# Retention and gated MLP in one kernel: b divided out of w_sg and put back at the output, the middle row tile of two batches mixed on TensorE's row halves, w_in loaded by SyncE in columns, and an engine listed for each cast and copy

## The chip, the cores and the metric

One core of one Trainium2 chip. The metric is the device time of one execution in microseconds (us), here the median of three runs; lower is better.

## The reference

q, k and v are f32 of 8 batches x 8 heads x 576 positions x 64. Each head's scores are masked and damped by a power of the distance, without softmax, and multiplied with v; the 8 heads side by side make x (8 x 576 x 512), which goes through a gated MLP that mixes over positions:

```
ret = (q @ k.T / 8) * Dmat            # Dmat = gamma_h ** (i - j) for j <= i, else 0
x   = concat_heads(ret @ v)
h   = gelu_tanh(x @ w_in)             # 512 -> 1024; u = h[:512], v = h[512:]
v_n = (v - mean) / sqrt(var + 1e-6) * g_ln
v_s = w_sg @ v_n + b_sg               # over positions, 576 x 576; b_sg one number a position
out = x + (u * v_s) @ w_out
```

## The kernel before, in words

**Tiles.** A pair of batches has 2 x 576 = 1152 rows, which are 9 row tiles of 128; tile 4 (MID) holds the last 64 rows of the one batch and the first 64 of the other. There are 4 pairs. The attention runs over 36 steps i of its own, 9 a pair: a step takes 256 rows of 4 heads (two such steps make two row tiles), or the middle tile of all 8 heads.

**Attention of a step.** SP loads q, k and v (L317). The damping is split into a factor on q and one on v: POOL multiplies q and v (L515, L518) and casts k to bf16 (L511; ACT does the first four, L509). PE transposes q and k (L531), DVE copies them out of PSUM (L534); from step 20 on the DMA transposes them instead (L523). PE makes the scores in 64x64 tiles (L556), DVE masks them (L570), PE multiplies with v (L689) and adds what earlier rows bring through a running state (L681; the state is summed by L589 and kept block diagonal in zbdA and zbdB, which ACT, DVE and POOL fill). This lands in p_oz, of which there is one; ACT copies it to xT (L719), x with its features on the partitions.

**MLP of a row tile.** mlp_V (L756): 4 matmuls of 512 columns with the second half of w_in (L762), gelu on ACT (L765), mean and variance on DVE (L770 to L772), the power -0.5 on POOL (L775), a last product on DVE (L777) and the normalised vn on ACT (L787). mlp_U (L791): the same with the first half of w_in, turned (L802), gelu to uT on ACT (L807). batch(b) (L812), once all vn of a batch are there: 8 groups of 5 matmuls of 288 columns mix the positions (L824), and DVE multiplies each with uT (L832). Of the middle tile each batch has only 64 rows; the other 64 rows of vmid hold 1/g_ln and the matching rows of wT hold b_sg, so that the same matmul brings the bias in (L405 to L439 make both, with transposes on PE). Then 4 matmuls of 512 columns with w_out a row tile (L851; g_ln is multiplied into w_out, L478). x is added in the first half of the tiles by 4 transposing matmuls on PE (L854), and ACT copies the sum out (L865); in the last 18 (late) the DMA transposes x (L844) and DVE adds it (L861). SP writes the tile (L869).

**Weights.** w_in comes by 4 DMAs that POOL issues and that cast on the way (L329). w_sg comes by SP (L445), POOL casts it (L447), PE transposes it in 25 pieces (L454), DVE and ACT copy them to wT (L460 to L466). A copy that is shifted by 64 rows, for the odd batches, is made by 3 DMAs from SBUF to SBUF (L469).

**What sets the order.** Every piece of work is a unit of the class Plan (L116): an engine, a planned cost, what it reads and writes. TURN (L19) gives each unit its place in one sequence by hand, and the units are issued in that sequence, so that on each engine the order is fixed. The planned costs only choose PSUM banks (4 of them, p_d, for all MLP work and the transposes) and put 30 matmuls on zeros (L292) into gaps at the start.

## Time and profile before

| what | value |
|---|---|
| runs | 209.09, 209.66, 211.18 us; median 209.66 |
| span of the profiled execution, first to last instruction | 208.7 us |
| mean granted TensorE clock | 0.992 |
| busy: PE, DVE, ACT, POOL | 197.3, 161.3, 136.9, 125.0 us |
| moved by DMA | 48.93 MB, 234 GB/s on average |

The profile is of one execution, whose span is 208.7 us; the runs' times are 0.4 to 2.5 us above that, since they also hold what lies ahead of the first and behind the last instruction and differ from run to run. PE is the engine of the matmuls and PEld its weight loads; a matmul's end is modelled, so the starts of rows, not their lengths, tell what one costs in a stream. DVE, ACT and POOL are VectorE, ScalarE and GpSimd; SPq is the queue of SyncE. "x4" in a row is the number of instructions that were merged into it.

### The profile page before, as it was taken

What the parts mean: (1) busy time and instruction counts of PE and PEld (TensorE: products, weight loads), DVE (VectorE), ACT (ScalarE), POOL (GpSimd) and SP (SyncE); (2) the same over time, 40 slices, a digit from 0 to 9 for tenths busy, and PEclk for the clock granted to TensorE, in tenths of its full rate; (3) what the DMA queues carried; (4) which work ended last, traced back from release to release, by engine and by line L of the source; (5) the groups of instructions that cost most, each with busy time, mean ns of one, the idle gap of its engine ahead of it and who ended that gap; (6) DMA issues with size and microseconds to landing.
All of it is one profiled execution on the core that took longest, in us unless ns stands there. A gap on an engine that the chain in (4) does not pass through costs nothing.

```text
span 208.7 us, 7251 instructions
## 1 busy us (share of the span) xinstructions
PE 197.3 (95%) x2892; PEld 127.1 (61%) x2892; DVE 161.3 (77%) x440; ACT 136.9 (66%) x304; POOL 125.0 (60%) x186
## 2 busy tenths in 40 slices
PE   7779799999997999999999999999999999999992
PEld 2354568668675676667565667566657556664651
DVE  1383969879997998877987798557999998787573
ACT  5428468886778448886578677994785498644400
POOL 4965999998991897853869229635766563103000
PEclk9969999999999999999999999999999999999999
DMA  5999999999999999999999997999999999697655
GB/s 160 302 188 254 224 284 305 289 314 275 193 219 223 316 279 284 300 266 230 131 327 221 204 195 225 132 239 273 249 208 259 216 221 189 136 316 181 175 162 216
DMA packets 99073, 48.93 MB, mean 234 GB/s; under 512 B 42848, under 2 KB 93344, under 8 KB 99040
## 3 DMA queue, kind: packets, MB, share of 16 engines
q1 hardware_dynamic: 97808, 47.30, 99.9%
q0 software_dynamic: 1088, 1.05, 3.4%
q8 instruction: 22, 0.36, 0.8%
q14 instruction: 11, 0.09, 0.2%
q10 hardware_dynamic: 144, 0.13, 0.2%
HBM read 32.79 MB, written 9.44 MB: 202 GB/s over the span
## 4 chain that ended last, share of the span: by engine, by line
PE 84%; POOL 4%; issue 3%; DMA 3%; DVE 2%; ACT 1%; SPq 1%; DVEq 0%; POOLq 0%
PE p_d L824 19%; PE p_d L851 15%; PE p_d L762 15%; PE p_d L802 14%; PE p_oz L689 5%; PE p_s L556 4%; PE p_d L531 3%; PE p_oz L681 3%; DMA qkf<-in_q_dram 3%; PE p_d L854 2%; PE p_oz L589 1%; SPq L317 1%; PE p_d L454 1%; POOL qkb L515 1%; DVE ret L570 1%
## 5 line engine op out<-in xcount | busy, mean ns | idle before, releaser
L570 DVE TENSOR_TENSOR ret<-p_s,tri 128x512 bf16<-128x512 f32 x64 | 42.5, 683 | 6.5 <-PE p_s L556 6.1
L775 POOL TENSOR_TENSOR stat<-stat,mhalf 128x1 f32<-128x1 f32 x36 | 19.8, 551 | 38.9 <-DVE stat L772 37.0
L515 POOL TENSOR_TENSOR qkb<-qkf,gq 128x512 bf16<-128x512 f32 x35 | 36.8, 1057 | 9.2 <-DMA qkf<-in_q_dram 9.2
L518 POOL TENSOR_TENSOR vb<-vf,gv 128x512 bf16<-128x512 f32 x36 | 37.9, 1058 | 6.4 <-DMA vf<-in_v_dram 5.7
L824 PE MATMUL p_d<-wT,vn 128*128 128x288 bf16 x256 | 40.6, 286 | 0.0
L802 PE MATMUL p_d<-xT,w_in 128*128 128x512 bf16 (+2 forms) x224 | 36.1, 303 | 0.0
L762 PE MATMUL p_d<-w_in,xT 128*128 128x512 bf16 x144 | 36.1, 380 | 0.0
L851 PE MATMUL p_d<-w_out,uT 128*128 128x512 bf16 (+1 forms) x148 | 35.9, 374 | 0.0
L719 ACT ACTIVATE xT<-p_oz 128x256 bf16<-128x256 f32 x64 | 24.4, 453 | 16.5 <-PE p_oz L689 11.1
L832 DVE TENSOR_TENSOR uT<-p_d,uT 128x288 bf16<-128x288 f32 x64 | 27.5, 452 | 9.4 <-PE p_d L824 8.0
L765 ACT ACTIVATE vg<-p_d 128x512 f32<-128x512 f32 x36 | 21.4, 595 | 15.7 <-PE p_d L762 14.9
L824 PEld LDWEIGHTS <-vn 128*128 128x128 bf16 x256 | 24.3, 98 | 8.2
L787 ACT ACTIVATE vn<-vg,stat 128x512 bf16<-128x512 f32 x32 | 25.6, 811 | 3.1 <-DVE stat L777 2.0
L770 DVE BATCH_NORM_STATS2 stat<-vg 128x6 f32<-128x512 f32 x36 | 24.6, 684 | 2.6 <-ACT vg L765 2.4
L807 ACT ACTIVATE uT<-p_d 128x512 bf16<-128x512 f32 x36 | 21.1, 594 | 6.0 <-PE p_d L802 5.8
L511 POOL CAST qkb<-qkf 128x512 bf16<-128x512 f32 x32 | 19.5, 612 | 9.1 <-PE p_oz L589 4.7
L802 PEld LDWEIGHTS <-w_in 128*128 128x128 bf16 x224 | 18.5, 98 | 10.3 <-issue 0.2
L851 PEld LDWEIGHTS <-uT 128*128 128x128 bf16 x148 | 13.9, 98 | 13.7
L762 PEld LDWEIGHTS <-xT 128*128 128x128 bf16 x144 | 13.0, 98 | 12.8 <-ACT xT L719 0.2
L534 DVE COPY qkT<-p_d 128x1024 bf16<-128x1024 bf16 x20 | 13.6, 682 | 6.4 <-PE p_d L531 6.2
L824 PE MATMUL p_d<-wT,vmid 128*128 128x288 bf16 x64 | 18.3, 287 | 0.0
L556 PE MATMUL p_s<-qkT 64*64 64x128 bf16 (+1 forms) x576 | 15.3, 218 | 3.1 <-DVE qkT L534 1.4
(96 smaller groups left out, 280.3 us busy)
## 6 DMA issues: line engine op xcount, KB each, us to landing
out_dram<-ob SPq DMA_DIRECT2D x35, 256.0 KB, 3.6
qkf<-in_q_dram SPq DMA_DIRECT2D x32, 256.0 KB, 5.6
qkf<-in_k_dram SPq DMA_DIRECT2D x32, 256.0 KB, 5.2
vf<-in_v_dram SPq DMA_DIRECT2D x32, 256.0 KB, 5.2
...
```

What stands on the lines that cost most here:

```text
L515: plan.add("POOL" if i else "DVE", 1010 if i else 700, key, lambda: eng.tensor_tensor(split(qs[a]), shape(qkf[l][:, 0, :]), gain(gq), op=A ...
L518: plan.add("POOL", 1010, key + 2, lambda: nc.gpsimd.tensor_tensor(shape(vb[a][:]), shape(vf[l][:]), gain(gv), op=Alu.mult), reads=rd(i, 2) ...
L556: nc.tensor.matmul(banks[hh][EA[e], j, :w] if n != MID else banks[hh][EA[e], kk // 2, kk % 2 * 64:kk % 2 * 64 + 64], qkT[r][EA[hh], 1, 2 * ...
L570: nc.vector.tensor_tensor(ret[r][hh][:].rearrange("p (s k j) -> p s k j", s=2, k=2), banks[0][:].rearrange("p (s k) j -> p s k j", s=2), t ...
L719: nc.scalar.activation(xT[p % NX][:, m + e, 2 * c:2 * c + 2, :].rearrange("p k (j s) -> p k s j", s=2), oz[:, e, :256].rearrange("p (k s j ...
L762: nc.tensor.matmul(banks[0][:], xT[p % NX][:, m, kk, :], w_in[:, kk, F2:], start=(kk == 0), stop=(kk == KK - 1))
L770: nc.vector.bn_stats(st[:, 0:6], vg[g][:])
L787: nc.scalar.activation(vn[p % 2][m][:], vg[g][:], Act.Identity, scale=st[:, 8:9], bias=st[:, 9:10])
L802: nc.tensor.matmul(hu[:, c, :].rearrange("p (t j) -> p t j", j=128), w_in[:, kk, 128 * (x * per + c):128 * (x * per + c) + 128], xT[p % NX ...
L824: nc.tensor.matmul(banks[0][:, :HS], src[:, 128 * c:128 * c + 128], wT[e][j][:, half * HS:(half + 1) * HS], start=(j == 0), stop=(j == SB ...
L832: plan.add("DVE", 380, key, lambda banks, c=c, col=col: nc.vector.tensor_tensor(uT[x][:, c, col:col + HS], banks[0][:, :HS], uT[x][:, c, c ...
L851: nc.tensor.matmul(banks[0][:, :w], uT[x][:, c, r], w_out[:, c, x0:x0 + w], start=(c == 0), stop=late and c == KK - 1, skip_group_check=True)
```

## The change

- **b.** POOL or ACT scales row t of w_sg by 1/b_sg[t] with the cast (wnat). What is mixed then lacks only 1/g_ln, which is a number a feature: the DVE instruction behind the mixing adds it and multiplies with uT (scalar_tensor_tensor). The output instruction multiplies each row with b_sg and adds x. The rows of 1/g_ln and b_sg in vmid and wT, their transposes and copies are gone, and vmid with them.
- **Output.** It is now on DVE for all 36 tiles, with x in rows (xr) ahead of it: in the first half by PE transposes (L920 of the new kernel) and a copy on ACT or DVE, in the second by DMA transposes of two tiles at a time (10 in place of 18). The transposes of q and k by the DMA are in pairs too (8 in place of 16).
- **Mixing.** mix(bs) in place of batch(b). The full tiles are 4 matmuls of 288 columns (L874), and the middle tile is one on 64 rows (L879): rows 0 to 63 for the even batch, 64 to 127 for the odd one. The first pair's batches are mixed apart; those of the other three pairs together, in 8 groups of 4 + 4 full matmuls and the two halves on two banks, once the whole pair is normalised.
- **State.** It is kept as it is summed, not block diagonal, and read in 64x64 tiles (L675); the part that crosses between the halves lands in further columns of p_oz. ACT copies that part to SBUF, ACT copies the rest to xT, and DVE adds the two where they meet. p_oz is free after that.
- **w_in.** Four column pieces as f32 by SP, two of them ahead of step 4's loads, staged in the output buffers and one new buffer, and cast by ACT or POOL. An mlp_V of the first two tiles runs in two halves.
- **Engines.** SIDE lists an engine for each cast and copy. From tile 10 on POOL does all the small steps of the norm. The shifted copy of wT is made by two copies on ACT and two on POOL. TURN is written anew.

The diff, cut to its core:

```diff
@@ SIDE, new: one letter for each call of a name, in order (P POOL, A ACT, D DVE) @@
+SIDE = {
+    "kb": "PAPPAPAPAAPPPPAPPPPAPPPAAPPPAPPAPAAP",
+    "qkT": "DAAADDAADDDAADADADAA",
+    "qs": "DPDDPPPDPPPPPPPPPPPPPPPPPPPPPPPPPPPP",
+    "vb": "DPPDPPPPDPPPPPPPPPPPDPPPPPPPPPDPPPPP",
...
+    "w_in": "PAAP",
...
+    "xr": "DADDDAADAD",
...
@@ Plan.add @@
+        if isinstance(engine, dict):
+            sides, some = engine, emit
...
+            engine = self.side[name][mine] if name in self.side else next(iter(sides))
...
@@ w_load @@
-        plan.add("POOL", 770, (1 - half) * T0 + 10 + c, lambda: nc.gpsimd.dma_start(
-            w_in[:, c:c + 2, half * F2:(half + 1) * F2],
...
+        plan.add("SP", 450, (1 - half) * T0 + 10 + c, lambda: nc.sync.dma_start(
+            part_, moe_w_in.rearrange("(k p) f -> p k f", p=128)[:, :, f0:f0 + F2 // 2]),
+            writes=[("wf", x)] + held, dma=1600)
+        plan.add({"ACT": 870, "POOL": 1140}, None, (1 - half) * T0 + 10 + c, lambda e: copy(
+            e, w_in[:, :, f0:f0 + F2 // 2], part_),
+            reads=[("wf", x)] + held, writes=[("w_in", half, c)])
...
@@ weights @@
-            plan.add("POOL", 625, kw, lambda j=j, n=n: nc.gpsimd.tensor_copy(wnat[:n, j, :], wsg[j][:n, :]), reads=[("wsg", j)], writes=[("wnat", j)])
+            plan.add({"POOL": 640, "ACT": 560}, None, kw, lambda e, j=j, n=n: copy(
+                e, wnat[:n, j, :], wsg[j][:n, :], b_inv[:n, j:j + 1]), reads=[("wsg", j), "gb_inv"], writes=[("wnat", j)])
...
-            plan.add("SP", 600, kw + 2 * T0, lambda dst=dst, src=src: nc.sync.dma_start(dst, src),
+            plan.add({"ACT": 150 + 430 * src.shape[1], "POOL": 60 + 620 * src.shape[1]}, None, kw + 2 * T0,
+                     lambda e, dst=dst, src=src: copy(e, dst, src),
...
@@ outp @@
-                    nc.tensor.matmul(oz[:, e, kk * w:kk * w + w], t[:, x, :], q_cols(r, n, kk, slice(0, 128), e),
-                                     start=not begun[e], stop=False, skip_group_check=True)
...
+            for crossed in range(2):
+                for x in range(2):
+                    for s, k, t, z in inter_of(i, x ^ crossed):
+                        at = 256 + s * w if crossed else (2 * s + x) * w
+                        put(x, k, at, t[EA[x], z, :], q_cols(r, n, s, k, EA[x], x ^ crossed))
...
+        plan.add("ACT", 270 if len(both) == 2 else 175, key + 8, crossed, reads=[("otu", i)],
+                 writes=[("xc", i % 2)], look=[(u, [0])])
+        plan.add("ACT", 425 if mid else 310 if len(both) == 2 else 460, key + 8, whole, reads=[("otu", i)] + after,
+                 writes=[("xT", p % NX, n)], look=[(u, [0])])
+        plan.add("DVE", 335 if len(both) == 2 else 200, key + 8, summed, reads=["ozS", ("xc", i % 2), ("xT", p % NX, n)],
+                 writes=[("xS", p % NX, n)], give=[(u, [0])])
...
@@ mix, in place of batch @@
-                    for j in range(SB):
-                        src = vmid[p % 2][e] if lo + j == MID else vn[p % 2][lo + j]
-                        nc.tensor.matmul(banks[0][:, :HS], src[:, 128 * c:128 * c + 128],
...
+                    for y, b in enumerate(bs):
+                        e = b % 2
+                        for t in range(MID):
+                            nc.tensor.matmul(banks[y][:, :HS], vn[p % 2][e * (MID + 1) + t][:, cols], wT[e][e + t][:, s0],
+                                             start=t == 0, stop=False, skip_group_check=True)
+                    for y, b in enumerate(bs):
+                        e = b % 2
+                        r = slice(e * NB0, e * NB0 + NB0)
+                        nc.tensor.matmul(banks[y][:, :HS], vn[p % 2][MID][r, cols], wT[e][0 if e else SB - 1][r, s0],
+                                         start=False, stop=True, skip_group_check=True)
...
-                plan.add("DVE", 380, key, lambda banks, c=c, col=col: nc.vector.tensor_tensor(
-                    uT[x][:, c, col:col + HS], banks[0][:, :HS], uT[x][:, c, col:col + HS], op=Alu.mult),
+                    plan.add("DVE", 380, key, lambda banks, c=c, col=col: nc.vector.scalar_tensor_tensor(
+                        uT[x][:, c, col:col + HS], banks[0][:, :HS], g_inv[:, c:c + 1], uT[x][:, c, col:col + HS],
+                        op0=Alu.add, op1=Alu.mult),
...
@@ project @@
-                    for kk in range(0 if late else w // 128):
-                        nc.tensor.matmul(banks[0][:, 128 * kk:128 * kk + 128], xT[x][:, m, x0 // 128 + kk, :], ident[:],
...
-                    plan.add("ACT", 500, key, lambda banks, o=o: nc.scalar.activation(ob[o][:], banks[0][:], Act.Copy),
...
+                plan.add("DVE", 610 if w == DM else 340, key, lambda banks, o=o, m=m, w=w, xa=xa, half=half, x0=x0: nc.vector.scalar_tensor_tensor(
+                    ob[o][:, :w], banks[0][:, :w], b_col[:, m:m + 1], xr[xa][:, half].rearrange("p k j -> p (k j)")[:, x0:x0 + w],
+                    op0=Alu.mult, op1=Alu.add),
...
@@ done @@
-        if (n == MID or n == U - 1) and b != 2 * NP - 3:
-            if b == 2 * NP - 2:
-                batch(b - 1)
-            batch(b)
+        if n == MID and p < APART:
+            mix([2 * p])
+        elif n == U - 1:
+            mix([2 * p + 1] if p < APART else [2 * p, 2 * p + 1])
```

Three places where the order moves. In the rows a name ends in the number of its buffer and of its allocation; wT0 and wT1 are w_sg turned for even and odd batches, vn0 and vn1 the normalised tiles of even and odd pairs.

PE, the end of one mixing group and the start of the next, second pair before:

```order
L824 LDWEIGHTS vn1_2_141
L824 MATMUL p_d3_180<-wT0_158,vn1_2_141 128x288
L824 LDWEIGHTS vn1_3_142
L824 MATMUL p_d3_180<-wT0_158,vn1_3_142 128x288
L824 LDWEIGHTS vmid1_0_150
L824 MATMUL p_d3_180<-wT0_158,vmid1_0_150 128x288
L824 LDWEIGHTS vn1_0_139
L824 MATMUL p_d2_179<-wT0_158,vn1_0_139 128x288
```

and the same pair in the change:

```order
L874 LDWEIGHTS vn1_8_141
L874 MATMUL p_d2_168<-wT1_150,vn1_8_141 128x288
L879 LDWEIGHTS vn1_4_137
L879 MATMUL p_d1_167<-wT0_149,vn1_4_137 128x288
L879 LDWEIGHTS vn1_4_137
L879 MATMUL p_d2_168<-wT1_150,vn1_4_137 128x288
L874 LDWEIGHTS vn1_0_133
L874 MATMUL p_d0_166<-wT0_149,vn1_0_133 128x288
```

The fifth matmul of 128 rows has become two of 64 rows on two banks, behind eight full ones.

SP, around the loads of w_sg, before:

```order
L317 DMA vf3_70<-in_v_dram 128x4x128
L317 DMA qkf4_65<-in_k_dram 128x4x128
L317 DMA qkf4_65<-in_q_dram 128x4x128
L317 DMA vf4_71<-in_v_dram 128x4x128
L445 DMA wsg1_118<-in_moe_w_sg_dram 128x576
L445 DMA wsg4_121<-in_moe_w_sg_dram 64x576
L445 DMA wsg0_117<-in_moe_w_sg_dram 128x576
L390 DMA b_col_163<-in_moe_b_sg_dram 128x4x1
L391 DMA b_col_163<-in_moe_b_sg_dram 64x1
L445 DMA wsg2_119<-in_moe_w_sg_dram 128x576
L445 DMA wsg3_120<-in_moe_w_sg_dram 128x576
```

and in the change, from w_in's first pieces to step 4, and from step 9 to w_sg:

```order
L358 DMA vf1_68<-in_v_dram 128x4x128
L374 DMA ob0_142<-in_moe_w_in_dram 128x4x256
L374 DMA ob1_143<-in_moe_w_in_dram 128x4x256
L350 DMA qkf2_63<-in_k_dram 64x8x64 x2
L350 DMA qkf2_63<-in_q_dram 64x8x64 x2
```

```order
L358 DMA qkf2_63<-in_q_dram 128x4x128
L358 DMA vf1_68<-in_v_dram 128x4x128
L453 DMA wsg1_112<-in_moe_w_sg_dram 128x576
L358 DMA vf2_69<-in_v_dram 128x4x128
L358 DMA qkf2_63<-in_k_dram 128x4x128
L453 DMA wsg4_115<-in_moe_w_sg_dram 64x576
L453 DMA wsg0_111<-in_moe_w_sg_dram 128x576
L453 DMA wsg3_114<-in_moe_w_sg_dram 128x576
L453 DMA wsg2_113<-in_moe_w_sg_dram 128x576
```

The last piece of w_sg has gone from SP's row 29 to row 45, and ahead of it now stand the four pieces of w_in.

POOL, before, between the loads of w_in and the casts of step 3:

```order
L518 TENSOR_TENSOR vb2_79<-vf1_68,gv_172 128x512
L329 DMA w_in_155<-in_moe_w_in_dram 128x2x512 x2
L395 TENSOR_SCALAR g_tmp_161<-g_col_160 128x4
L396 TENSOR_SCALAR g_inv_162<-g_col_160 128x4
L397 TENSOR_TENSOR g_tmp_161<-g_tmp_161,g_inv_162 128x4
L398 TENSOR_TENSOR g_col_160<-g_col_160,g_tmp_161 128x4
L515 TENSOR_TENSOR qkb3_76<-qkf0_61,gq_171 128x4x2x64
L518 TENSOR_TENSOR vb3_80<-vf0_67,gv_172 128x512
```

and in the change, at the same steps:

```order
L332 CAST qkb1_74<-qkf1_62 128x2x4x64
L527 TENSOR_TENSOR vb2_77<-vf1_68,gv_161 128x512
L332 CAST w_in_146<-ob0_142 128x4x256
L332 CAST zsA1_96<-s2_0_93 128x128
L332 CAST zsB0_97<-s1_0_91 128x128
L524 TENSOR_TENSOR qkb0_73<-qkf2_63,gq_160 128x4x2x64
L524 TENSOR_TENSOR qkb0_73<-qkf3_64,gq_160 128x2x4x64
L527 TENSOR_TENSOR vb0_75<-vf2_69,gv_161 128x512
```

The four small steps on g (g_tmp to g_col) have gone from the middle of the first steps to a later place, and one cast of w_in stands there instead.

650 lines of the change are left out of this document (345 added, 305 removed), and 109 rows, old and new, of the table TURN.

## The prediction

> **What bounds the kernel now.** I read the page first, then busy time by stage, then the chain and PE's rows in order of time.
>
> ```profile
> span 208.7 us, 7251 instructions
> PE 197.3 (95%) x2892; PEld 127.1 (61%) x2892; DVE 161.3 (77%) x440; ACT 136.9 (66%) x304; POOL 125.0 (60%) x186
> PE 84%; POOL 4%; issue 3%; DMA 3%; DVE 2%; ACT 1%; SPq 1%; DVEq 0%; POOLq 0%
> 0.00:45.76 45.76, 39.60 (x606) 25.17 (x607) 28.95 (x80) 29.16 (x73) 37.54 (x74) 0.96 1.06 255
> 68.00:204.90 136.90, 136.86 (x1896) 86.60 (x1894) 112.20 (x308) 91.03 (x193) 71.30 (x92) 1.00 1.05 229
> 204.90:208.70 3.80, 0.00 (x0) 0.00 (x0) 0.47 (x2) 0.00 (x0) 0.00 (x0) 1.00 0.53 190
> ```
>
> (Columns of the last three: stretch, length, busy PE, PEld, DVE, ACT, POOL with counts, granted clock, DMA share, GB/s.) From 68 to 204.9 PE is busy throughout at full clock, while DVE has 24.7 us free. What changes the time there is the length of PE's own stream, and a new wait of PE. The last 3.8 us are the last output's way out, and they stay. The first 45.76 us, up to the first mixing, are different: POOL is busy 82% of them, and PE's 39.6 us hold the fill matmuls, slow isolated ones and gaps. So there are two sums: PE's stream, and what is lost before the first mixing.
>
> **PE's stream.** What a matmul costs in a stream is the distance of the starts.
>
> ```profile
> 139.97 0.65 PE L824 MATMUL p_d<-wT,vn 128*128 128x288 bf16 x4
> 140.46 0.29 PE L824 MATMUL p_d<-wT,vmid 128*128 128x288 bf16 x1
> 140.58 0.65 PE L824 MATMUL p_d<-wT,vn 128*128 128x288 bf16 x4
> 142.42 0.28 PE L681 MATMUL p_oz<-qkT,zbdB 128*128 128x128 bf16 x2
> 142.62 0.42 PE L689 MATMUL p_oz<-ret,vb 64*64 64x128 bf16 x16
> 142.99 0.40 PE L556 MATMUL p_s<-qkT 64*64 64x128 bf16 x16
> 143.32 1.04 PE L762 MATMUL p_d<-w_in,xT 128*128 128x512 bf16 x4
> 144.19 0.65 PE L824 MATMUL p_d<-wT,vn 128*128 128x288 bf16 x4
> 38.44 0.28 PE L454 MATMUL p_d<-ident,wnat 128*128 128x128 bf16 x2
> 38.64 0.20 PE L454 MATMUL p_d<-ident,wnat 64*128 64x64 bf16 x1
> 38.77 0.28 PE L454 MATMUL p_d<-ident,wnat 128*128 128x128 bf16 x2
> ```
>
> A mixing group of five takes 140.58 - 139.97 = 0.61 us, 0.122 each or 0.424 ns a column; four of 512 columns take 0.87 us by the same rate. A 128-column matmul is thus 0.054 us. The rows also price a change of the tile layout. Two L681 from 142.42 are through at 142.53, yet the 64x64 ones start at 142.62: 0.09 us. Sixteen L556, four at once, are through at 142.99 + 4 x 0.054 = 143.21, and L762 starts at 143.32: 0.11 us. The case that matters is 64 rows by all 128 columns, which is L879's layout, and L454 has it: two transposes from 38.44 end their stream at 38.55, the 64-row one starts at 38.64 (0.09), streams 64 columns to 38.67, and the next full one starts at 38.77 (0.10). So going to 64 rows and back costs some 0.2 us. The Trainium skill, TensorEngine Tiling (Array Packing), Tiling Modes, says that a change of tiling mode drains the engine; this trace agrees with its 0.09 to 0.11 us.
>
> - Mixing, streamed. In three pairs, 24 groups have 9 slots where two groups had 10; the halves write two banks from two row halves, as L689's quarter tiles do side by side, so the second is free: -24 x 0.12 = -2.9 us. The 16 groups of the first pair keep 5 slots.
> - Mixing, changes of layout. The 40 groups each leave the full layout for the half rows. In 7 the attention's 64x64 work stands right behind, so the way back is shared. Counted over both orders, 86 changes before become 157: 71 x 0.10 = **+7.1 us**. A joined pair of groups takes 8 x 0.122 + 0.122 + 0.20 = 1.30 us where two took 1.22.
> - State. In the 24 steps with both parts, 4 full matmuls (0.22 us) become 8 quarter ones, four at once (0.11): -2.6 us. The others stay about level. They now stand behind the layout change instead of ahead of it, which is one change either way.
> - Gone: nine transposes for g and b, 9 x 0.054 = -0.5 us. The turning of x on PE is 72 matmuls of 128 columns both ways.
>
> The sum is +1.1 us. At the lower bound the changes cost nothing, -6.0; at the upper the halves also don't run side by side, +4.0. I take +1.1, since L454's four places are the same layout.
>
> **The start.** Here the chain leaves PE.
>
> ```profile
> GB/s 160 302 188 254 224 284 305 289 314 275 193 219 223 316 279 284 300 266 230 131 327 221 204 195 225 132 239 273 249 208 259 216 221 189 136 316 181 175 162 216
> 19.51 0.24 POOL L395 TENSOR_SCALAR g_tmp<-g_col 128x4 f32<-128x4 f32 x1 [2.32 <-ACT g_tmp L906]
> 20.57 1.06 POOL L515 TENSOR_TENSOR qkb<-qkf,gq 128x512 bf16<-128x512 f32 x1
> 24.88 1.91 PE L802 MATMUL p_d<-xT,w_in 128*128 128x256 bf16 x16
> 28.85 1.06 SPq L445 DMA_DIRECT2D wsg<-in_moe_w_sg_dram  x2
> 38.31 1.45 PE L454 MATMUL p_d<-ident,wnat 128*128 128x128 bf16 x15
> 45.72 0.53 PE L824 MATMUL p_d<-wT,vn 128*128 128x288 bf16 x3
> L292 PE MATMUL p_d<-zero 128*128 128x512 bf16 x30 | 10.0, 464 | 1.2 <-DVE zero L890 1.2
> ```
>
> Ahead of the first mixing (45.7) the order has, at the prices above and without the 30 fills, 24.9 us of PE work: 7 tiles of mlp_V, 64 matmuls of mlp_U, the transposes and attention of 7 to 9 steps, w_sg's transposes. So 20.8 us are lost there. One loss is plain: POOL stands 2.32 us for ACT, because the warm-up of the gelu table writes g_tmp (L906), then spends 1 us on g, and only then makes step 3's q. In the change the warm-up has a tile of its own and the steps on g come later. Of each later step, part of the casts lies on ACT and DVE (4 of the first 9 k, 4 q and 3 v), and POOL no longer issues w_in's four DMAs.
>
> The new order has 32.1 us of work ahead of its first mixing: 10 tiles of mlp_V, 72 of mlp_U, 12 steps' transposes, 9 sets for x. Its time is set by what SP loads first. By the diff's shapes, from SP's first row to w_sg's last piece (row 45) it is 12.1 MB, w_in's 2.1 MB in f32 among them. The GB/s row sums to 2320 over its first nine slices of 5.22 us, 12.1 MB at 47.0 us; without w_in's casting DMA (slices 3 and 5 are the slow ones) it might be 293, the mean of slices 6 to 10: 2.4 MB at 10.4, 43.5 for all. I take 46.5. Behind that come one cast of w_sg, 25 transposes and a copy, about 3 us. The first mixing is then at 49.5, with 49.5 - 32.1 = 17.4 us lost: **-3.4 us** against 20.8. The ends: -4.6, since mlp_U waits for its piece of w_in (row 26, 7.6 MB, so about 29 to 31 instead of 24.88) and 16 us are lost by then; +1.5, if the last cast comes at 51.5.
>
> **What lies beside PE.**
>
> ```profile
> L861 DVE TENSOR_TENSOR ob<-p_d,xr 128x512 f32<-128x512 f32 x17 | 11.5, 684 | 1.3 <-PE p_d L851 1.3
> L565 DVE TENSOR_TENSOR ret<-p_s,tri_mid 128x256 bf16<-128x256 f32 x8 | 3.2, 414 | 0.1
> L638 DVE TENSOR_TENSOR s<-p_oz,s 128x128 f32<-128x128 f32 x12 | 3.4, 286 | 4.4 <-PE p_oz L589 3.3 <-ACT vmid L784 1.0
> L515 DVE TENSOR_TENSOR qkb<-qkf,gq 128x512 bf16<-128x512 f32 x1 | 1.1, 1061 | 2.6 <-DMA qkf<-in_q_dram 2.6
> L534 DVE COPY qkT<-p_d 128x1024 bf16<-128x1024 bf16 x20 | 13.6, 682 | 6.4 <-PE p_d L531 6.2
> L658 DVE TENSOR_TENSOR zbdA<-p_oz,s 64x128 bf16<-64x128 f32 x36 | 10.2, 284 | 0.2
> L777 DVE TENSOR_SCALAR stat<-stat 128x1 f32<-128x1 f32 x36 | 7.2, 205 | 1.0 <-POOL stat L775 1.0
> L772 DVE TENSOR_SCALAR stat<-stat 128x1 f32<-128x1 f32 x36 | 5.5, 154 | 1.3
> L719 ACT ACTIVATE xT<-p_oz 128x256 bf16<-128x256 f32 x64 | 24.4, 453 | 16.5 <-PE p_oz L689 11.1 <-DVE zbdA L658 2.6 <-DVE zbdA L632 2.5
> 67.54 0.30 PE L556 MATMUL p_s<-qkT 64*64 64x128 bf16 x5 [1.41 <-issue]
> ```
>
> DVE gains 18 outputs (x 0.684 = 12.3), 24 sums of 256 and 12 of 128 columns (13.4, at L565's and L638's prices), 8 products for q and v (8.5 at L515's), 6 copies of x (3.7). It gives up 11 copies of qkT (7.5), 26 times two steps of the norm (9.3), the block-diagonal writes (about 15) and what made g's and b's rows (about 3): +3 us on 161.3. The added scalar operand of its 101 outputs and mixings has no row alone; L777 (two scalars of a tensor) against L772 (none) bounds it by 0.05 each, 5 us. That leaves some 35 us free. POOL gets the 52 small steps at L395's 0.24 (12.5 us) in a stretch where it has 65 us free, and ACT gives up 18 output copies for the crossed parts. None of this is on PE's path, so I cost it at nothing. Its price if the cover goes is in the last rival. The 1.41 us of issue at 67 are a wait for nothing that the trace shows, and I keep them. At the end 8 joined mixings and 9 projections stand behind the last norm, 18 us of PE work with 14 us of DVE work: covered.
>
> Sum: +1.1 - 3.4 = -2.3 us on the span, 206.4. The median of the runs is 1.0 above that span, so **207.4 us** (209.66 before).
>
> **The rivals.**
>
> *The halves cost no change of layout.* Then the stream is 6 us shorter and the time is 209.7 - 6.0 - 3.4 = 200.3. For it: two row halves side by side are what L689 shows. Against it: L454's 0.09 and 0.10 us at each of its places, and nothing that could hide them. Chance 0.15. The Trainium skill, TensorE: Matmul & The Clock Gate, Part 3, gives a pack of tiles the span of one matmul and about 4 ns for each further tile, with no price for getting into it; by that the mixing would gain 2.9 us and this rival holds, and L454's rows speak against it.
>
> *The start gives nothing.* w_sg's last cast comes behind other work on POOL, the first mixing is at 52 to 53, and PE runs dry instead of standing behind POOL: 209.7 + 1.1 - 1 to 0 = 209.8 to 210.8. For it: 16 more SP rows ahead, and the rate of 254 and less while w_in came. Chance 0.2.
>
> *p_oz is held too long* (slower). Before, ACT alone frees the one p_oz, by two copies. In the change DVE frees it, behind both ACT copies and in DVE's own order, and what is queued behind the waiting PE instruction is all of the MLP. One more DVE instruction of 0.41 and whatever DVE is at, mostly 0.68, come on top. If PE meets this in half of the 27 joined steps for 0.5 us, it is 7 us: 209.7 - 2.3 + 7 = 214.4. It decides from 4.4 us on, 0.16 us a joined step. For it: DVE is busy 82% from 68 on. Against it: between two steps PE has some 3.5 us of MLP work, and the loop is about 3. Chance 0.2.
>
> **How the numbers follow.** The forecast has 0.45, with a range of its own from 205.5 to 209.5; a bit over half of it lies over 1% below 209.66, about what a measurement of this kernel can tell from no change. Faster: 0.25 + 0.15 + 0.05 of milder mixtures = 0.45. Within 1%: the rest of the forecast and the second rival, 0.37. Slower: the last, 0.18. The range of 202 to 212.5 leaves out most of the first rival and the end of the last, about 0.2.
>
> **What would show it.** A joined mixing of 1.30 us in the rows, 0.2 of it at the half rows (1.11 for the first rival). The first mixing between 48 and 51. PE without idle time after it, but for an issue wait or two (waits of L675 for DVE in the last rival). mlp_U's first rows at 29 to 31. DVE near 165 us busy. I am wrong if the first mixing is later than 52, if PE's idle time after it passes 3 us, or if the half rows cost under 0.1.

## The result, and the profile after

The changed kernel takes 217.69 us (median of 4 runs, 215.56 to 218.24), the kernel before beside it 209.41 us: a ratio of 1.039, with a 95% interval of 1.032 to 1.046. It is **slower by some 8 us**, where 207.4 us was forecast. The profiled execution has a span of 216.5 us, against 208.7. Ratios compare undisturbed runs of both kernels; where too few of a kernel were left, only its median is given.

The page of the changed kernel, and three stretches of it and one of the kernel before (columns as in the prediction):

```profile
span 216.5 us, 7451 instructions
PE 196.2 (91%) x2984; PEld 117.1 (54%) x3019; DVE 169.0 (78%) x383; ACT 134.4 (62%) x300; POOL 136.3 (63%) x226
PE 43%; DMA 17%; SPq 11%; ACT 10%; POOL 9%; DVE 4%; issue 3%; DVEq 0%; POOLq 0%; ACTq 0%
0.00:55.80 55.80, 45.69 (x850) 30.51 (x860) 40.77 (x100) 39.59 (x98) 40.85 (x65) 1.00 1.02 259
107.00:180.00 73.00, 68.89 (x1039) 39.93 (x1051) 58.38 (x131) 41.77 (x94) 43.86 (x80) 1.00 1.05 230
```

```profile
107.00:180.00 73.00, 73.00 (x1070) 45.60 (x1068) 59.18 (x170) 54.87 (x116) 41.81 (x55) 1.00 1.12 220
```

The chain that ends last is no longer PE's: PE has 43% of it, where it had 84%, and loads, SP, ACT and POOL have most of the rest. From 107 to 180 PE was busy all the 73 us; now 4 us are missing. (Some of that is records that the trace lacks, 30 of 300 on two lines, each a hole of exactly one 0.216 us matmul. Of the 4.1 us missing, 3.0 are waits.) What PE waited for behind its first mixing, with the sum, the number and the longest, is listed here by its five largest lines; all of these waits are 4.2 us, where the kernel before has one stand of 1.4:

```profile
PE p_oz L675 <- POOL zsB L332: 1.4, 1, 1.4
PE p_d L537 <- DVE xr L332: 0.7, 1, 0.7
PE p_oz L675 <- DVE xT L755: 0.7, 1, 0.7
PE p_d L537 <- DVE uT L890: 0.5, 1, 0.5
PE p_s L562 <- DMA qkT<-qkb: 0.4, 1, 0.4
```

Each is put down to another engine or to a DMA, not to PE. The joined mixing itself is as it was forecast:

```profile
113.48 1.14 PE L874 MATMUL p_d<-wT,vn 128*128 128x288 bf16 x8
114.55 0.30 PE L879 MATMUL p_d<-wT,vn 64*128 64x288 bf16 x2
114.78 1.15 PE L874 MATMUL p_d<-wT,vn 128*128 128x288 bf16 x8
```

From 113.48 to the next group at 114.78 it is 1.30 us. The change of layout costs 0.095 us on the way into the half rows and 0.104 on the way back, and the two halves start 3 ns apart (means over the groups behind 75 us).

**Where the 7.8 us of span arise.** Ahead of the first mixing the prediction counted 24.9 us of PE work before and 32.1 after. It starts at 55.8 now, so 55.8 - 32.1 = 23.7 us are lost, against 20.8: +2.9. Behind it, PE's order at the prediction's prices holds 147.8 us, against 154.9, so the whole stream is about as long as it was (+0.1). From the first mixing to PE's last matmul it took 212.27 - 55.84 = 156.4 us, against 204.59 - 45.59 = 159.0; with 0.1 for that last one, 8.7 us are lost, against 4.2: +4.5. Together 7.5. The listed waits make up 2.8 of the 4.5 (4.2 against 1.4); the rest shows in this count alone.

The start, in the rows of PE, POOL and SP (the last is the landing time of the five pieces of w_sg, from issue):

```profile
34.23 1.92 PE L852 MATMUL p_d<-xT,w_in 128*128 128x256 bf16 x16 [0.62 <-POOL w_in L332]
43.82 1.74 POOL L334 TENSOR_SCALAR wnat<-wsg,gb_inv 128x576 bf16<-128x576 f32 x1
47.12 5.12 POOL L334 TENSOR_SCALAR wnat<-wsg,gb_inv 128x576 bf16<-128x576 f32 x3
52.30 2.29 PE L463 MATMUL p_d<-ident,wnat 128*128 128x128 bf16 x23 [0.52 <-POOL wnat L334]
55.84 0.65 PE L874 MATMUL p_d<-wT,vn 128*128 128x288 bf16 x4
L453 SPq DMA_DIRECT2D wsg<-in_moe_w_sg_dram x5: 429/586/809, 37.9 to 41.7; - x5
DMA to landing us min/median/max: 4.9/6.2/6.5
```

w_sg is there at about 41.7 + 6.5 = 48.2. The casts that divide by b take 1.72 us each on POOL, where the plain cast took 0.66, and three stand behind each other up to 52.2.

### The profile page after: what moved, and what is told of

The parts are those of the page before. It is cut to its first block, busy times and chain, and to the rows that moved or that the text cites. A ratio compares the mean times of both kernels' runs of the same rounds, so it can differ in the third digit from the quotient of the medians.

```text
span 216.5 us, 7451 instructions
## 1 busy us (share of the span) xinstructions
PE 196.2 (91%) x2984; PEld 117.1 (54%) x3019; DVE 169.0 (78%) x383; ACT 134.4 (62%) x300; POOL 136.3 (63%) x226
## 4 chain that ended last, share of the span: by engine, by line
PE 43%; DMA 17%; SPq 11%; ACT 10%; POOL 9%; DVE 4%; issue 3%; DVEq 0%; POOLq 0%; ACTq 0%
PE p_d L874 11%; PE p_d L933 8%; PE p_d L807 6%; PE p_d L852 6%; DMA vf<-in_v_dram 6%; SPq L358 5%; DMA qkT<-qkb 4%; SPq L350 4%; DMA wst<-in_moe_w_in_dram 3%; PE p_oz L675 3%; POOL vb L527 3%; PE p_d L879 3%; DMA qkf<-in_k_dram 3%; ACT vn L837 3%; POOL wnat L334 2%
## 5 line engine op out<-in xcount | busy, mean ns | idle before, releaser
L524 POOL TENSOR_TENSOR qkb<-qkf,gq 128x512 bf16<-128x512 f32 x32 | 33.2, 1043 | 11.4 <-DMA qkf<-in_q_dram 9.3
L890 DVE SCALAR_TENSOR_TENSOR uT<-p_d,gb_inv,uT 128x288 bf16<-128x288 f32 x64 | 30.9, 511 | 10.4 <-PE p_d L879 8.9
L527 POOL TENSOR_TENSOR vb<-vf,gv 128x512 bf16<-128x512 f32 x31 | 32.2, 1042 | 10.0 <-DMA vf<-in_v_dram 8.3
L874 PE MATMUL p_d<-wT,vn 128*128 128x288 bf16 x256 | 38.2, 287 | 0.0
L807 PE MATMUL p_d<-w_in,xT 128*128 128x512 bf16 (+1 forms) x135 | 34.4, 367 | 3.1 <-issue 0.6
L837 ACT ACTIVATE vn<-vg,stat 128x512 bf16<-128x512 f32 x36 | 29.1, 814 | 7.0 <-POOL stat L830 6.4
L938 DVE SCALAR_TENSOR_TENSOR ob<-p_d,gb,xr 128x512 f32<-128x512 f32 (+1 forms) x37 | 26.6, 730 | 2.4 <-DMA out_dram<-ob 0.9
L874 PEld LDWEIGHTS <-vn 128*128 128x128 bf16 x256 | 22.9, 98 | 9.8
L332 POOL CAST qkb<-qkf 128x512 bf16<-128x512 f32 x23 | 14.3, 623 | 7.4 <-DMA qkf<-in_k_dram 6.6
L827 POOL TENSOR_SCALAR stat<-stat 128x1 f32<-128x1 f32 x26 | 5.9, 228 | 19.8 <-DVE stat L820 13.8
L537 PE MATMUL p_d<-ident,qkb 128*128 128x128 bf16 x160 | 13.0, 224 | 2.6 <-POOL qkb L524 0.9
```

Source lines behind the costliest of these rows:

```text
L524: plan.add({"POOL": 1010, "DVE": 700}, None, key, lambda e: by[e].tensor_tensor(split(qs[a]), shape(qkf[l][:, 0, :]), gain(gq), op=Alu.mul ...
L527: plan.add({"POOL": 1010, "DVE": 700}, None, key + 2, lambda e: by[e].tensor_tensor(shape(vb[a][:]), shape(vf[l][:]), gain(gv), op=Alu.mul ...
L807: nc.tensor.matmul(banks[0][:, y * w:y * w + w], xT[p % NX][:, m, kk, :], w_in[:, kk, F2 + y * w:F2 + y * w + w], start=(kk == 0), stop=(k ...
L837: plan.add("ACT", 720, key + 2, lambda: nc.scalar.activation(vn[p % 2][m][:], vg[g][:], Act.Identity, scale=st[:, 8:9], bias=st[:, 9:10]), ...
L874: nc.tensor.matmul(banks[y][:, :HS], vn[p % 2][e * (MID + 1) + t][:, cols], wT[e][e + t][:, s0], start=t == 0, stop=False, skip_group_chec ...
L890: plan.add("DVE", 380, key, lambda banks, c=c, col=col: nc.vector.scalar_tensor_tensor(uT[x][:, c, col:col + HS], banks[0][:, :HS], g_inv[ ...
```

## The experiments

Each was timed beside the kernel before on the same chip (medians of 209.4 to 210.7 us, so gains of a microsecond read off the medians are rough). Runs that put edits together are named by the edits.

| run | median us (lowest to highest) | ratio to before, 95% |
|---|---|---|
| the change | 217.69 (215.56 to 218.24) | 1.039 (1.032 to 1.046) |
| e1 no division | 216.66 (215.26 to 217.78) | 1.032 (1.025 to 1.039) |
| e2 division on DVE | 226.87 (221.91 to 229.27) | - |
| e3 middle tile full | 216.25 (212.40 to 218.23) | 1.019 (1.008 to 1.031) |
| e4 e2 and e3 | 223.92 (220.62 to 225.13) | 1.057 (1.047 to 1.067) |
| e5 no scaling on POOL | 216.32 (214.75 to 216.72) | 1.023 (1.017 to 1.030) |
| e6 w_in by POOL | 228.72 (224.84 to 229.21) | - |
| e7 no scalar operands | 218.67 (216.20 to 219.35) | 1.035 (1.027 to 1.043) |
| e8 e3, e5 and e7 | 213.48 (213.15 to 216.65) | 1.012 (1.006 to 1.018) |
| e9 turned copies by SP | 231.69 (230.99 to 234.60) | 1.105 (1.100 to 1.109) |
| e10 w_in by POOL, early | 217.08 (215.94 to 220.03) | 1.034 (1.030 to 1.039) |
| e11 e3 and e9 | 229.23 (225.74 to 232.11) | 1.083 (1.075 to 1.091) |
| e12 e3, e9 and e10 | 229.29 (228.26 to 231.30) | 1.096 (1.088 to 1.103) |
| e13 turned copies on ACT's queue | 218.71 (217.46 to 222.58) | 1.043 (1.037 to 1.048) |
| e14 e3, e13, w_out on ACT | 222.36 (221.15 to 224.89) | 1.066 (1.058 to 1.074) |
| e15 single transposes | 235.26 (232.98 to 236.37) | 1.122 (1.114 to 1.130) |
| e16 e14 and e15 | 235.87 (234.57 to 238.72) | 1.124 (1.118 to 1.131) |
| e17 half loads | 214.59 (214.11 to 214.97) | 1.027 (1.019 to 1.035) |
| e18 e8 and e17 | 209.50 (208.58 to 210.14) | 1.003 (0.999 to 1.007) |

### The division by b, and the half rows (e1 to e4)

e1 leaves the scale out of w_sg's casts:

```diff
-                e, wnat[:n, j, :], wsg[j][:n, :], b_inv[:n, j:j + 1]), ...
+                e, wnat[:n, j, :], wsg[j][:n, :]), ...
```

> The change with one operand left out: the casts of w_sg no longer divide by b, so the output lacks that division; all else is as in the change. In the change each full cast takes 1.72 us on POOL (4 of them, one 64-row one on ACT at 0.75), where the plain cast before took 0.64. Theory 1 (the price of the division): the three casts that end at 52.2 end 3.2 us earlier, but w_sg's last piece lands at about 48.2, so the first mixing moves from 55.8 to 51.5-52.5, and 1 us of POOL behind it is saved for the next steps; the kernel takes 212.5 to 214.5 instead of 217.7. Rival (the loads bind): the first mixing comes earlier, but PE's waits behind it (some 5 us between 64 and 179, for POOL, DVE and the DMA transposes) grow by the same; 216.5 to 218.

It came out 1.0 us under the change (1.6 by the ratios), and the first mixing moved by 0.6 only, to 55.25. The casts are indeed cheap again and done at 49.8:

```profile
L332 POOL CAST wnat<-wsg x4: 660/669/670, 44.0 to 49.1; 128x576 bf16<-128x576 f32 x4
L463 PE MATMUL p_d<-ident,wnat x25: 199/219/243, 51.6 to 53.8; 128*128 128x128 bf16 x16, 64*128 64x64 bf16 x4, 128*64 128x128 bf16 x4, 64*64 64x64 bf16 x1
```

But PE comes to the transposes of w_sg only at 51.6: what its order puts ahead is late by itself. The price is real, but most of it was hidden behind a delay that was there anyway. Theory 1 falls.

e2 puts the division on DVE:

```diff
-    "wnat": "PPPPA",
+    "wnat": "DDDDD",
...
-            plan.add({"POOL": 640, "ACT": 560}, None, kw, lambda e, j=j, n=n: copy(
+            plan.add({"POOL": 640, "ACT": 560, "DVE": 400}, None, kw, lambda e, j=j, n=n: copy(
```

> The change with all five divisions of w_sg by b put on DVE instead of four on POOL and one on ACT. DVE's price for 128x576 f32 to bf16 with a scalar of a column has no row yet; from its 0.41 to 0.68 us for 256 and 512 columns out of PSUM I estimate 0.4 to 0.75. Theory 1: POOL loses 6.9 us of work in front of the first mixing, which moves from 55.8 to 51-52.5; 212 to 214.5, as in the run without the division or up to 1 us better. Rival (the loads bind): 216.5 to 218. A third case: DVE is the busy one there (93% from 40 to 50), and the 2 to 4 us on DVE hold masks and sums of the next steps: 215 to 217.

Its single runs take 221.9 to 229.3 us, 4 to 12 above the change's median, and not for the price. The rows, of a run of 226.4 us, are DVE's cast, the wait ahead of it, and PE's wait:

```profile
L334 DVE TENSOR_SCALAR wnat<-wsg,gb_inv x5: 512/604/1302, 42.9 to 56.2; 128x576 bf16<-128x576 f32 x4, 64x576 bf16<-64x576 f32 x1
  DMA wsg<-in_moe_w_sg_dram: 5.4, 2
PE p_s L562 <- DVE qkT L332: 6.7, 2, 6.3
```

DVE takes 0.60 us in the median (0.51 to 1.30), under POOL's 1.72. But at these places in the order DVE stands 5.4 us for w_sg to land, a copy of qkT is queued behind it, and PE waits 6.3 us for that copy. PE is 8.5 us later than in the change from there on, and still 8.3 us later at the end: in this run nothing behind 60 us gives the delay back.

e3 mixes the middle tile in full matmuls. The rows that the other batch has in the tile meet zeros in the weights, so the result is the same:

```diff
+            nc.vector.memset(wTs[0][NB0:, SB - 1, :], 0.0)
+            nc.vector.memset(wTs[1][:NB0, 0, :], 0.0)
...
-                        r = slice(e * NB0, e * NB0 + NB0)
-                        nc.tensor.matmul(banks[y][:, :HS], vn[p % 2][MID][r, cols], wT[e][0 if e else SB - 1][r, s0],
+                        nc.tensor.matmul(banks[y][:, :HS], vn[p % 2][MID][:, cols], wT[e][0 if e else SB - 1][:, s0],
```

> The change with the middle tile mixed in full 128-row matmuls: the unused 64 rows of the two weight tiles are zeros written once at the start, so the other batch's rows add nothing and the result is the same. A joined pair of groups then is 10 matmuls of 288 columns without a change of layout, 10 x 0.122 = 1.22 us instead of 1.30, a single one 0.61 instead of 0.81. Over PE's whole order that is 4.4 us less by the rows' prices. Theory 1 (half rows cost 0.2 us a visit, and PE is still the engine that sets the time from the first mixing on): 217.7 - 4.4 = 213.3, between 212.5 and 214.5. Rival (from the first mixing on PE waits for loads, POOL and DVE): the gaps of PE grow by what the stream loses, 216.5 to 217.7.

> Both at once: the division on DVE and the full 128-row middle tile. Theory 1: the two gains add, 3.2 to 5 and 4.4 us: 208 to 210, level with the kernel before. Rival (loads, POOL and DVE bind behind the first mixing): well under the sum of the two single gains, 213 or more.

e3 gains, by 1.4 us in the medians and 2% in the ratios, with single runs far apart. In its trace the stretch from the first mixing to PE's last matmul is 2.5 us shorter, where the stream lost 4.4; the other 1.9 became waits. One of them, near 172 us, the change's trace does not have:

```profile
PE p_d L854 <- ACT uT L859: 1.7, 1, 1.7
```

e4 shares the 6 us stand of DVE with e2, and shows no sure gain over it: their quickest runs are 220.6 and 221.9 us. So far it is open between the two: the length of PE's stream counts, but nearly half of what it lost turned into waits.

### Prices on POOL and DVE, and the way of w_in (e5 to e8, e10)

e5 also casts w_out without its scale. e7 makes DVE's two instructions plain. e8 is e5, e7 and e3 together:

```diff
-                    e, w_out[:, c + r, :], obs[s][:, r, :], g_col[:, c + r:c + r + 1]), ...
+                    e, w_out[:, c + r, :], obs[s][:, r, :]), ...
```

```diff
-                    plan.add("DVE", 380, key, lambda banks, c=c, col=col: nc.vector.scalar_tensor_tensor(
-                        uT[x][:, c, col:col + HS], banks[0][:, :HS], g_inv[:, c:c + 1], uT[x][:, c, col:col + HS],
-                        op0=Alu.add, op1=Alu.mult),
+                    plan.add("DVE", 380, key, lambda banks, c=c, col=col: nc.vector.tensor_tensor(
+                        uT[x][:, c, col:col + HS], banks[0][:, :HS], uT[x][:, c, col:col + HS], op=Alu.mult),
...
-                    op0=Alu.mult, op1=Alu.add),
+                    ob[o][:, :w], banks[0][:, :w], xr[...], op=Alu.add),
```

> The change with both weights cast plainly: w_sg without the division by b and w_out without the product with g, so the output lacks these two. In the change a scaled cast on POOL takes 1.72 us (w_sg, 4 of them) and 1.57 us (w_out, 3), where the order was drawn up for 0.64 and 0.62; plain they take 0.67. The run without the division alone came out 1 us under the change. Theory 2 (the order was made for cheaper instructions, and PE's late waits come of POOL and DVE being behind it): 7 us less on POOL, of which 3 behind the first mixing; 213 to 215.5, against 217.7. Theory 3 (the DMA queues are full from 10 to 70 us, at 1.02 to 1.20 of the 16 engines' time, and data come late whatever POOL does): 216 to 217.5.

> The change with DVE's two new scalar operands left out: the mixing's result is multiplied by u without adding 1/g, and the output is the projection plus x without the product with b, so the output lacks both. An instruction then costs as in the kernel before: 372 ns instead of 429 (64 of them) and 608 instead of 663 (36), 5.6 us of DVE's 169. Theory 2: DVE stands ahead of PE's waits at 64, 80 and 151 us; 214 to 216. Rival: DVE has slack there and the waits are for what DVE itself waits for; 217 to 218.

> The change with plain weight casts, without DVE's scalar operands and with full 128-row mixing of the middle tile: every price that the prediction or the order had too low is gone, at the cost of the division by b, the product with g, the added 1/g and the product with b at the output. Theory 2: PE is busy without gaps again from the first mixing on, and its stream is 4.4 us shorter; 217.7 - 4.4 - 4 to 5 of waits = 208 to 210. Theory 3 (loads and their queues set when things are ready): the shorter work turns into waits for loads, 212.5 to 215.

e5 is 1.4 us under the change (3.3 by the ratios): POOL's scaled casts cost something, most of it in the start, where the first mixing comes at 54.6. e7 is no faster at all: DVE's 5.6 us are covered, as the prediction had it. e8 is 2.8 us under e5, but PE still waits some 6 us behind its first mixing. The two largest:

```profile
PE p_d L854 <- ACT uT L859: 1.4, 1, 1.4
PE p_oz L677 <- POOL zsB L332: 1.2, 1, 1.2
```

Theory 2, that the order is only too cheaply priced, falls with it.

e6 and e10 load w_in by POOL's casting DMA again, without SP's four rows and the four casts. e6 issues it at SP's places in the common order, e10 as early as the kernel before has it:

```diff
-        plan.add("SP", 450, (1 - half) * T0 + 10 + c, lambda: nc.sync.dma_start(
-            part_, moe_w_in...[:, :, f0:f0 + F2 // 2]),
+        plan.add("SP", 450, (1 - half) * T0 + 10 + c, lambda: nc.gpsimd.dma_start(
+            w_in[:, :, f0:f0 + F2 // 2], moe_w_in...[:, :, f0:f0 + F2 // 2]),
...
-            e, w_in[:, :, f0:f0 + F2 // 2], part_),
+            None),
```

```diff
+ in e10, behind the masks on POOL: w_piece(1, 0), w_piece(1, 1); at the V half's old places: w_piece(0, c)
+        nc.gpsimd.dma_start(w_in[:, :, f0:f0 + F2 // 2], moe_w_in...[:, :, f0:f0 + F2 // 2])
```

> The change with one part undone: w_in is again loaded by POOL's casting DMA straight into its bf16 tile, in the same four column pieces and at the places in the order where SP issued them; SP loses four rows, ACT and POOL the four casts of 1.04 us. Theory 3 (loads and SP's queue): w_sg leaves SP some 2 to 3 us earlier (four rows at 0.5 to 0.8 us and their place in the full queues), the casts of w_in no longer stand ahead of q and k; PE has 1 to 2 us more done at 48 us, and the time is 213.5 to 216. Rival (POOL's DMA is as slow here as before, 254 GB/s and less while it ran, and 0.8 to 1 us of POOL for each issue): 216.5 to 219.

> The change with w_in loaded by POOL's casting DMA, this time issued where the kernel before has it: the V half right behind the masks (about 7 us), the U half where the V half stood (about 16), instead of 17 and 37 us as in the run before this one, where PE waited 5.9 and 5.6 us for it. Theory 3 (w_in through SP in f32 makes the start late): mlp_V starts at 17 instead of 18.65, mlp_U is no longer waited for, w_sg leaves SP 2 us earlier; the first mixing moves from 55.8 to 53-54.5 and 215 to 216.5 is left. Rival: POOL, which is busy from 9 to 56, loses 0.9 us for each issue and gets only the two casts of 1.04 back, and the order of PE does not let mlp_U come earlier; 217 to 218.5.

e6 is worse by 7 to 12 us in its single runs, because POOL is at those places only at 17.4 and 37.5 us, where SP was at 10.7 and 26.1. PE's waits, and PE's busy time with the granted clock behind it:

```profile
PE p_d L806 <- DMA w_in<-in_moe_w_in_dram: 5.9, 1, 5.9
PE p_d L851 <- DMA w_in<-in_moe_w_in_dram: 5.6, 1, 5.6
20.00:30.00 10.00, 5.24 (x64) 0.53 1.03 215
```

While PE stands, its clock goes down to a mean of 0.53. The Trainium skill, TensorE: Matmul & The Clock Gate, Part 1, has the array at half clock after one idle window of about 3.4 us; the row's 0.53 agrees with the half, and does not show the length of the window. e10, without these waits, is level with the change within its spread, its first mixing is at 56.0, and mlp_U starts at 35.2. The 1.9 us that PE waits for casts of w_in in the change are gone, but it waits 3.9 for q and k on POOL, where the change has 0.9:

```profile
PE p_d L541 <- POOL qkb L528: 2.2, 1, 2.2
PE p_d L541 <- POOL qkb L332: 1.7, 1, 1.7
```

So w_in by POOL's DMA brings nothing back; what its way by SP costs alone, e10 does not tell.

### The turned copies of w_sg (e9, e11 to e14)

In the change the copies for the odd batches are two instructions on ACT (1.16 and 1.64 us) and two on POOL; before they were transfers. e9 makes them SP's transfers at the same places, e13 two on ACT's own queue where ACT had its first copy. e14 adds to e13 and e3 that w_out's casts are all on ACT:

```diff
-                     lambda e, dst=dst, src=src: copy(e, dst, src),
+                     lambda e, dst=dst, src=src: nc.sync.dma_start(dst, src),
```

```diff
+        nc.scalar.dma_start(wTs[1][NB0:], wTs[0][:NB0])
+        nc.scalar.dma_start(wTs[1][:NB0, 1:], wTs[0][NB0:, :SB - 1])
...
-                    e, w_out[:, c + r, :], obs[s][:, r, :], g_col[:, c + r:c + r + 1]),
+                    "ACT", w_out[:, c + r, :], obs[s][:, r, :], g_col[:, c + r:c + r + 1]),
```

> The change with one part undone: the copies of the turned w_sg for the odd batches, which in the change are two copies on ACT (1.16 us at 60.5, 1.64 at 76.5) and two on POOL (1.14 each), are SBUF-to-SBUF transfers on SP's queue again, at the same four places in the order. Theory 4 (the copies stand ahead of ACT's small copies of the attention, DVE then stands 1.3 and 1.5 us for ACT at 62 and 77, and PE for DVE, 0.64 at 64.5 and 0.81 at 80.4): these two waits of PE go, and 1.4 to 1.5 us with them; 216 to 216.5 against 217.7. Rival (those waits are of DVE's own making, or SP's queue stands for the transfers): no gain, 217 to 219.

> The change with the copies of the turned w_sg as two SBUF-to-SBUF transfers, issued on ACT's own queue where ACT had its first copy (60.5 us), so that they land some 10 us ahead of their use at 79. ACT loses 2.8 us of copies and pays for two issues, POOL loses 2.3 us. Theory 4: PE's waits at 64.5 and 80.4 (0.64 and 0.81) go, the step at 82 us is 1 to 1.5 us earlier, and 215.5 to 216.7 is left. Rival: DVE's other work holds PE there just as long; 217 to 218.5.

e9 does not test this: SP reaches those places only at 76 and 87 us, and PE waits for the transfers themselves. e13 does what was meant, yet is no faster. PE's wait at 80.4 is gone, the one at 64 stays, and another has come. Here are e9's wait, e13's new one, and where it comes from:

```profile
PE p_d L874 <- DMA wT<-wT: 14.8, 2, 10.1
```

```profile
PE p_d L937 <- POOL w_out L334: 2.1, 1, 2.1
70.77 1.57 POOL L334 TENSOR_SCALAR w_out<-ob,gb 128x512 bf16<-128x512 f32 x1 [5.74 <-DMA ob<-in_moe_w_out_dram]
```

The transfers land 8.7 and 9.5 us after their issue. The second load of w_out, issued beside them, lands at 70.7, where it landed at 65.9 in the change, and POOL stands 5.74 us for it. Theory 4 holds for the second wait alone, and the gain goes into a load.

> The change with the turned copies as transfers and the middle tile mixed in full 128-row matmuls over zero rows (result unchanged). Theory 4: the two gains add, 1.4 and 2 to 4: 212.5 to 214.5. Rival (new waits take their place): 215 or more.

> The change with w_in by POOL's DMA at the early places, the turned copies as transfers and full 128-row mixing. If all three theories hold: 217.7 - 1.4 - 1.5 - 3 = 211 to 212.5, still above the kernel before at 209.5 to 210.5 by what is left of the start and the wait at 124 us; if the loads bind, 213.5 to 215.5.

> The change with full 128-row mixing over zero rows, the turned copies as transfers on ACT's queue, and the three scaled casts of w_out that POOL has (1.57 us each) on ACT (0.71 each) at the same places in the order; the result is the reference's. Theory 4 with the measured gains: 217.7 - 3 - 1.4 - 0.5 to 1 = 212 to 213. Rival (what is gained turns into waits for loads): 214 to 216.

e11 and e12 carry e9's waits for the transfers, 13 to 14 us, and tell nothing more. In e14 the casts of w_out on ACT stand in front of the gelu, and ACT waits for the same load:

```profile
66.87 0.72 ACT L330 ACTIVATE w_out<-ob,gb 128x512 bf16<-128x512 f32 x1 [6.49 <-DMA ob<-in_moe_w_out_dram]
```

### Loads and SP's queue (e15 to e18)

In the change as before, SP's queue issues the loads of q, k and v, the outputs and, here from 92 us on, the DMA transposes. The waits that stand on it, of the kernel before and of the change (the largest of each line):

```profile
SPq L523 <- POOL vb L518: 8.7, 5, 3.5
SPq L523 <- POOL stat L775: 8.0, 4, 3.5
SPq L869 <- DVE ob L861: 6.9, 8, 2.0
```

```profile
SPq L944 <- DVE ob L938: 18.8, 15, 5.4
SPq L497 <- POOL stat L827: 9.5, 2, 5.5
SPq L497 <- POOL vb L527: 5.5, 2, 3.7
SPq L497 <- POOL zsA L332: 5.3, 1, 5.3
```

All rows of the transposes of q and k together are 38.1 us of waiting against 23.7 before, and the outputs 18.8 against 6.9. A pair can go only when both steps are cast; an output, when DVE has made it. The loads stand behind. They leave late, but do not take longer: by the pages, v lands some 5.2 us after its issue before, and 5.3 in the change. The v of step 23 is issued at 105 us instead of 93, and its scores are wanted at 111 instead of 119. Two steps on, this ends in PE's longest wait:

```profile
117.06 1.16 SPq L358 DMA_DIRECT2D vf<-in_v_dram  x2
124.22 1.04 POOL L527 TENSOR_TENSOR vb<-vf,gv 128x512 bf16<-128x512 f32 x1 [3.21 <-DMA vf<-in_v_dram]
125.55 0.25 PE L675 MATMUL p_oz<-qkT,zsB 64*64 64x128 bf16 x4 [1.43 <-POOL zsB L332]
```

The page's "POOL zsB" hides it: that copy of 0.29 us stood on POOL behind a v product that stood for a load.

e15 splits the pairs:

```diff
-            plan.add("SP", 1300, i * T0, lambda: nc.sync.dma_start(qkTs[r]..., qkbs[a]..., transpose=True),
+            plan.add("SP", 1300, i * T0, lambda: single(i + 1),
...
+ behind the later of the casts of step i's q and k: single(i)
```

> The change with the DMA transposes of q and k one step at a time (16 in place of 8 pairs); the first of a pair stands in SP's queue right behind the casts of its own step, the second where the pair stood. Theory 5 (SP stands 2.9 to 5.9 us in one pair and the loads behind it come late: the v load for 124 us is issued behind the pair of 110.1, the wait at 153 is for the pair of 144.8): the waits of PE behind 110 us, some 3 us, shrink by 1 to 2; 215.5 to 216.7. Rival: a transpose takes SP as long per block alone as in a pair, and the loads come as late; 217 to 218.5.

> The three parts of the run before the last and single transposes. If both theories hold: 210.5 to 212, at best level with the kernel before (209.4 to 210.7); if neither holds beyond the half rows: 214 to 216.

These two tell nothing of the theory. In e15 PE stands 5.4 us for a transpose ahead of the products that read q (p_oz). Read from the order, and not shown, the first transpose of a pair now stands ahead of products of an earlier step that still read the same buffer, so that they take the new data and other waits arise. A split that keeps the order of the readers was not tried.

e17 leaves every instruction where it is and takes half of the bytes out of the loads from step 8 on; e18 does so in e8:

```diff
-                             dst[:].rearrange("p (h f) -> p h f", h=HU),
-                             src[2 * p + e, c * HU:c * HU + HU, r0:r0 + 256, :]...
+                             dst[:].rearrange("p (h f) -> p h f", h=HU)[:, :HU // few],
+                             src[2 * p + e, c * HU:c * HU + HU // few, r0:r0 + 256, :]...
```

> The change with half of the bytes of q, k and v loaded from step 8 on (two of four heads, the rest of a buffer keeps old data, so those heads are wrong): 10.5 of 28.3 MB of loads less, every instruction at its place. Theory 3 (DMA queues that are full make data late, and PE's waits behind the first mixing follow): w_sg lands 2 to 3 us earlier, PE's waits at 124 and 151-153 go, 211 to 214 against 217.7. Rival (order and prices of the engines themselves): 216 to 218.

> The run with plain casts, no scalar operands and full 128-row mixing (213.5), now with half of the loads' bytes from step 8 on as well; outputs are wrong in what these leave out. Theory 3: the waits that were left in it (61.9, 77.6, 120, 135, 148, 168: 7 us) shrink to 2 or 3, and 208 to 210 is left. Rival: 212 to 214.

All of PE's waits behind its first mixing in e17, and the stretch that lacked 4 us of PE:

```profile
PE p_d L537 <- DVE xr L332: 0.7, 1, 0.7
PE p_d L537 <- DVE uT L890: 0.5, 1, 0.5
PE p_d L807 <- ACT uT L857: 0.2, 1, 0.2
107.00:180.00 73.00, 72.79 (x1114) 41.57 (x1113) 61.83 (x138) 44.32 (x101) 46.29 (x86) 1.00 0.83 185
```

Every wait behind 108 us is gone, at a DMA share of 0.83 instead of 1.05, and the time is 3.1 us shorter (2.6 by the ratios). By the count used above PE loses 4.9 us behind the first mixing, against 8.7 in the change and 4.2 before. **So the loss behind the first mixing is late loads, nearly all of it.** Two waits for DVE (uT and xr, 1.2 us) stay.

The start did not move (56.4), and w_sg's last piece landed at 47.8 instead of 48.2, not 2 to 3 us earlier. Nor does e17 show what makes the loads late. In it SP waits as long as in the change, 20.5 us for outputs and 35.3 for the transposes. But the loads land sooner, here those of v before, in the change and in e17, and a pair of transposes holds SP for 1.7 to 3.9 us instead of 2.9 to 5.9:

```profile
vf<-in_v_dram SPq DMA_DIRECT2D x32, 256.0 KB, 5.2
vf<-in_v_dram SPq DMA_DIRECT2D x32, 256.0 KB, 5.3
vf<-in_v_dram SPq DMA_DIRECT2D x27, 128.0 KB, 3.6
```

Full DMA queues alone are not it either: from 107 to 180 the kernel before has a share of 1.12, above the change's 1.05, and no wait. That outputs and transposes on SP's queue make the loads late is read from the rows; no run took them off that queue.

e18 now helps to tell what the half rows cost, since PE is busy in both. Its mixing, and its whole list of waits behind the first mixing:

```profile
112.77 1.15 PE L876 MATMUL p_d<-wT,vn 128*128 128x288 bf16 x8
113.75 0.41 PE L880 MATMUL p_d<-wT,vn 128*128 128x288 bf16 x2
113.99 1.03 PE L809 MATMUL p_d<-w_in,xT 128*128 128x512 bf16 x4
PE p_d L539 <- DVE uT L891: 1.1, 1, 1.1
PE p_d L539 <- DVE xr L332: 1.0, 1, 1.0
```

A joined group takes 1.22 us instead of 1.30, and a single one no change of layout. Over the order that is 4.4 us. e18 is 5.1 us under e17, and 4.9 in the spans, 208.4 against 213.3: 0.9 of it ahead of the first mixing and 3.7 from there to PE's last matmul, of the 4.4. It also has plain casts and no scalar operands; full rows and half loads alone were not run. In e3 and e8, where loads bind, part of the 4.4 went into waits. e18 is level with the kernel before, and it leaves out work; no run that computes the reference came under that kernel.

## Why the prediction was wrong, point by point

- **PE's stream, +1.1 us: right.** 1.30 us for a joined group was forecast and measured, at 0.095 and 0.104 us a change of layout. By the same prices the built order is as long as before, 1 us better than summed. The Trainium skill's drain (TensorEngine Tiling (Array Packing), Tiling Modes) agrees with these rows, and the first rival, by which the change of layout is free, is refuted.
- **The start, -3.4 us: wrong by 6.3.** The step was that the time of the first mixing "is set by what SP loads first", with 3 us behind the last piece. The last piece was 1.7 us later than forecast (48.2 for 46.5), and 7.6 us lay behind it. The prediction counted one cast at the old price; three scaled ones were queued on POOL. The second rival had the direction, a last cast behind other work on POOL, but put the first mixing at 52 to 53. And even with plain casts it still came at 54.0 to 55.5 (e1, e5, e8, e18); with half of the loads' bytes from step 8 on it came at 56.4 (e17), and with w_in by POOL at 56.0 (e10). PE comes to w_sg's transposes late by itself. Its waits ahead of the first mixing are 9.2 us, against 5.7 before, all short; 1.9 for w_in's casts, 1.6 at p_oz and 0.5 for w_sg's casts are new. In e10 the first of these are gone and others grew. Which edit makes the start late is **still open**. That mlp_U would start at 29 to 31 also failed: it started at 34.2, and at 35.2 with w_in loaded early.
- **"None of this is on PE's path, so I cost it at nothing": wrong by 4.5.** It held for most of DVE's work (169.0 us against 165 forecast, and e7 no faster). It failed for the loads and for SP, whose queue the prediction followed through the start only. Two moved steps issue DMAs there: outputs that now all wait for DVE, and transposes in pairs. What stood behind them, the loads, was never asked for. That late loads make the loss is shown by e17; that these two steps make the loads late is read from SP's rows.
- **The slow slices before.** The prediction put them to w_in's casting DMA. The changed kernel has such a slice too, 187 GB/s in its fourth, with w_in on SP, and there the middle tile's short rows are loaded. Its first nine slices sum to 2350, against 2320 before: the 293 GB/s were not to be had.
- **The last rival, p_oz held too long, was slower for another reason.** PE's waits for the sums that free p_oz are 1.6 us in all, not 7.
- **The falsifiers.** Of the three, two came true: a first mixing later than 52, and more than 3 us of PE idle behind it.
